# Two eighths of a V unit are kept across the layers, and parts of w_down lie elsewhere

## Chip, core and metric

The kernel runs on one core of one Trainium2 chip. The metric is the device time of one execution in microseconds, as the median of several runs. The profile is of one execution; its times are microseconds from the start of the span.

## What is computed

Two blocks are applied in turn, twice: x grows by grouped-query attention over a cached K and V, then by a SwiGLU feed-forward block (FFN). Both layers use the same weights and the same caches. There is one query token in each of 4 batches.

```python
B, Sq, D = 4, 1, 512
Hq, Hkv, Sk, Dh = 32, 8, 8192, 128        # A: attention, all bfloat16
F = 1792                                  # B: FFN

def _A_ref(x, k_cache, v_cache, wq, wo):
    q = (x @ wq).reshape(B, Sq, Hq, Dh).transpose(0, 2, 1, 3)
    k = jnp.repeat(k_cache, rep, axis=1)
    v = jnp.repeat(v_cache, rep, axis=1)
    scores = jnp.einsum("bhqd,bhkd->bhqk", q, k) * (Dh ** -0.5)
    p = _softmax(scores, axis=-1)
    o = jnp.einsum("bhqk,bhkd->bhqd", p, v)
    return o.transpose(0, 2, 1, 3).reshape(B, Sq, Hq * Dh) @ wo

def _B_ref(x, w_gate, w_up, w_down):
    return (_silu(x @ w_gate) * (x @ w_up)) @ w_down

x = A_x
x = x + _A_ref(_layernorm(x), ...)
x = x + _B_ref(_layernorm(x), ...)
x = x + _A_ref(_layernorm(x), ...)
x = x + _B_ref(_layernorm(x), ...)
```

## The kernel before

**Units and slots.** K and V are cut into 16 units (NP), each a pair of KV heads of one batch. K(L, u) and V(L, u) are the 4 MB of unit u that layer L reads. A unit fills one slot of SBUF, 32 KB in each of 128 partitions. There are four slots (0 to 3), and a fifth, QS, which holds wq until layer 1's projection is done and K or V after that. A slot has eight parts of 512 KB (NB = 8, `BW` elements wide; the code's index q), named `s<slot>.<q>`. They are called eighths here, and pairs where two are meant. All lie in the one tensor `kvf`, so the profile's DMA rows show `kvf` for K, V and the FFN's weights alike.

**Order of units.** Layer 0 takes units 0 to 15. Layer 1 takes 15, 14, 13, 12 and then 0 to 11, because some of the last units of layer 0 are still there: K(15), V(15) and V(14) whole (`keep`), and the last two eighths of K(13), which stand in PSUM during the FFN (`hold`).

**Loads.** All loads are issued by the sync engine (SP) from one list, `cmds`, strictly in order; `pump` issues the next one as soon as the parts of the slot that it fills are in `free`. `freed` adds parts and calls `pump`; it is called where the code emits the last reader of these parts, and SP itself then waits on semaphores for that reader. Every load and every recorded operation goes through `_Sync`, so the trace shows SP's loads on one line, L93.

**A unit's work.** DVE turns K with 32-bit transposes in its place (`turn`, L488; two eighths at a time except for the first and last unit of a layer). PE makes scores (`scores`, L512: four matmuls for an eighth), which ends with `finished`, and so frees the eighth. When the eighth eighth is scored, DVE takes the maximum (`max_p`, L518), PE transposes it (`max_t`, L523), and DVE, PE and ACT go on to the exponentials (`exps`). DVE turns the probabilities into the tile `pT` (`turn_p`, L576), and PE multiplies them with V (`values`, L644; half of the unit's V at a time is freed). Each engine runs its instructions in the order in which they are emitted. PE's work stands in the list `blocks`, and `drain(lag)` emits from its front while more than `lag` us (by the code's own estimates, 0.9 for a block) stand in it; the lag is `LAG` (2.0), and `AHEAD` for the second unit of layer 1. DVE's turns are emitted at once, and so ahead of the PE blocks in the list, and of the DVE work that those blocks call for.

**The change of layers.** The weights of layer 0's FFN are loaded into slot 1 (`W_SLOT[0]`) when V(0,13) has been used there. In elements of a partition: w_gate at 0 to 7168, the rest of w_up to 9216 (the larger part of w_up has a place of its own, `wres`), w_down's 14 blocks of 512 up to 16384, the slot's end. The last two of these (12 and 13) come late, by the command `W+`: their place holds the turned probabilities of the layer's last unit (`late_pT`), which POOL sets to zero first. Then `ffn` frees slot 1 piece by piece, and K(1,14) is loaded into these pieces: eighths 0 to 2 after the gate's matmuls (L882), 3 after w_up's, 4 and 5 after w_down's first eight blocks (L913), 6 and 7 after the rest. K(1,13) goes to QS, in two commands, after the projection (L841) and after what was held in PSUM is turned back (L453). K(1,12) goes to slot 0 in pairs as K(1,15) is scored there, and V(1,13) to slot 1 in two halves as K(1,14) is scored.

```python
cmds += [(("W", 0), W_SLOT[0], 0, NB), (("W+", 0), W_SLOT[0], NB, NB + 1)]
cmds += [(K(1, us[1]), s, a, b) for a, b in ((0, 3), (3, 4), (4, 6), (6, NB))]
cmds += [(K(1, us[2]), QS, 0, NB // 2), (K(1, us[2]), QS, NB // 2, NB - 2)]
cmds += placed(seq, ring, {0: twos, 1: half, len(seq) - 1: ends})
```

Of the kernel before, what the change touches and what calls it, by code (L numbers as in the profile page):

```python
# [9 lines left out]
FP32 = mybir.dt.float32  # L10
# [93 lines left out]
def bass_interleave_layers__gqa_block_cached__swiglu_ffn__decode_kernel(  # L104
# [40 lines left out]
    with ExitStack() as es:  # L145
# [13 lines left out]
        wo_sb = sb("wo_sb", [P, Hq, D], BF16)  # L159
        WDS = (((0, 8, 4), (8, 12, 4), (12, 14, 2)), ((0, 8, 2), (8, 12, 2), (12, 14, 2)))  # L160
        NW = len(WDS[0])

        W_SLOT = (1, 3)
        O_WU = KT * F
        O_WD = O_WU + KT * F - RES
        assert O_WD + FO * D <= SL
        wres = kvf[:, (NSLOT + 1) * SL:]

# [18 lines left out]
        def wd_at(s, fo, k):  # L187
            return columns(s * SL + O_WD + fo * D + pick2(k).start)

        pT_w = TB * NH * QB  # L190
        assert all((w[-1][1] - w[-1][0]) * D >= pT_w for w in WDS)

        def late_pT(s):
            return kvf[:, (s + 1) * SL - pT_w:(s + 1) * SL]

# [18 lines left out]

        pT = sb("pT", [P, TB, NH, QB], BF16)

        pb = sb("pb", [P, SW], BF16)
# [135 lines left out]
        for n, i in ((4, 0), (7, 1), (10, 2), (13, 3)):  # L353
            cmds.insert(n, (("wo", i), None, 0, 0))
        cmds += [(("W", 0), W_SLOT[0], 0, NB), (("W+", 0), W_SLOT[0], NB, NB + 1)]

        us = order[1]
        s = W_SLOT[0]
        cmds += [(K(1, us[1]), s, a, b) for a, b in ((0, 3), (3, 4), (4, 6), (6, NB))]
        cmds += [(K(1, us[2]), QS, 0, NB // 2), (K(1, us[2]), QS, NB // 2, NB - 2)]  # L360
        seq = loads(1, 3)
        ring = (0, 1, 3, QS, 2)
        cmds += placed(seq, ring, {0: twos, 1: half, len(seq) - 1: ends})
        assert W_SLOT[1] == ring[len(seq) % len(ring)]
        cmds += [(("W", 1), W_SLOT[1], 0, NB), (("W+", 1), W_SLOT[1], NB, NB + 1)]

        free = {(s, q) for s in range(NSLOT) for q in range(NB)}
# [3 lines left out]
        def load_weight(name, i=0, s=0):  # L371
# [5 lines left out]
            elif name == "wo":  # L377
                src = A_wo[i * H2 * Dh:(i + 1) * H2 * Dh, :]
                T.dma("sp", wo_sb[:, i * H2:(i + 1) * H2, :].rearrange("p (c j) n -> p c (j n)", j=NA),
                      src.rearrange("(c p j) n -> p c (j n)", p=P, j=NA), sem_w["wo"][i], writes=[f"wo{i}"])  # L380
            else:
                w0 = kvf[:, s * SL:(s + 1) * SL]
                if name == "W+":
                    load_wd(w0, i, NW - 1, ["late"])
                    return
                T._wait("pool", T._need((), [f"s{s}.{NB - 1}"]))
                T.op("pool", lambda e: e.memset(late_pT(s).bitcast(FP32), 0.0), writes=["late"])
                T.dma("sp", w0[:, 0:KT * F].rearrange("p (c x) -> p c x", c=2),
                      B_w_gate.rearrange("(c p e) f -> p c (e f)", c=2, e=2), sem_w["wg"][0],
                      writes=[f"s{s}.{q}" for q in range(NB)] + ["wg"])  # L390
                up = B_w_up.rearrange("(c p e) f -> c p (e f)", c=2, e=2)
                if i == 0:
                    T.dma("sp", wres[:, 0:2 * F], up[0], sem_w["wu"][0], writes=["wu0"])
                    T.dma("sp", wres[:, 2 * F:], up[1, :, 0:FY], sem_w["wu"][1], writes=["wu1"])
                T.dma("sp", w0[:, O_WU:O_WD], up[1, :, FY:], sem_w["wu"][2], writes=["wu2"])

                for j in range(NW - 1):
                    load_wd(w0, i, j)

        def load_wd(w0, L, j, also=()):  # L400
            a, b, e_ = WDS[L][j]
            T.dma("sp", w0[:, O_WD + a * D:O_WD + b * D].rearrange("p (m x) -> p m x", x=e_ * D),
                  B_w_down[a * P:b * P, :].rearrange("(m p e) n -> p m (e n)", p=P, e=e_), sem_w["wd"][j],
                  writes=[f"wd{j}"] + list(also))

        def pump(most=len(cmds)):
            while issued[0] < most:
                it, s, a, b = cmds[issued[0]]
                if it[0] == "wo":
                    load_weight(*it)  # L410
                else:
                    need = {(s, q) for q in range(a, b)}
                    if not need <= free:
                        return
                    free.difference_update(need)
                    if it[0] in ("W", "W+"):
                        load_weight(it[0], it[1], s)
                    else:
                        slot_of[it] = s
                        load(it, a, b, sem_s[s] if b - a == NB else part_sem())  # L420
# [4 lines left out]
        def load(it, a, b, sm):  # L425
            kind, L, u = it
            s = slot_of[it]
            gp, bt = pair_gb(u)
            src = (A_k_cache if kind == "K" else A_v_cache)[bt, 2 * gp:2 * gp + 2, :, :].rearrange(
                "h (p t) d -> (h p) (t d)", t=TT)  # L430
            over = [w for i, w in enumerate(WQ) if s == QS and a // (NB // 2) == i and w not in q_gone]
            q_gone.update(over)
            T.dma("sp", kv[:, s, a * BW:b * BW], src[:, a * BW:b * BW], sm,
                  writes=[f"s{s}.{q}" for q in range(a, b)] + over)

# [23 lines left out]
        def finished(it, a, b):  # L459
# [3 lines left out]
            if it in keep:  # L463
                slot_of[keep[it]] = slot_of[it]
                if it[0] == "K":
                    turned.update((1, it[2], q) for q in range(a, b))
            else:
                freed(slot_of[it], a, b)

# [14 lines left out]
        def turn(L, u, q, n):  # L484
            s = slot_of[K(L, u)]
            w = kv[:, s, q * BW:(q + n) * BW].bitcast(FP32)
            names = [f"s{s}.{i}" for i in range(q, q + n)]
            T.op("dve", lambda e: e.transpose(w, w), reads=names, writes=names)  # L488
# [16 lines left out]
        def scores(L, u, q):  # L505

            s = slot_of[K(L, u)]
            bk = SBK[turn_of[u]]
            w = kv[:, s, q * BW:(q + 1) * BW].rearrange("p (t c i e) -> p t c i e", t=TB, c=2, e=2)
            for c in range(4):  # L510
                z0 = ZP + c * P - REP * q
                T.op("pe", lambda e: e.matmul(bank(bk)[:, 0:SW], lhsT=zq[:, z0:z0 + P], rhs=w[:, :, c // 2, :, c % 2],  # L512
                                              start=(q == 0 and c == 0), stop=(q == NB - 1 and c == 3)),
                     reads=[f"s{s}.{q}", "zq"], writes=[f"pb{bk}"], sig=(c == 3))

# [50 lines left out]
        def pT_of(L, u):  # L566
            if u == order[L][-1]:
                return late_pT(W_SLOT[L]).rearrange("p (t n x) -> p t n x", n=NH, x=QB), "late"
            return pT[:], "pT"
# [17 lines left out]
        LAG = 2.0  # L587
        AHEAD = 15.0

# [37 lines left out]
        def values(L, u):  # L627
# [22 lines left out]
            def part(i):  # L650
# [18 lines left out]
                if i == 3:  # L669
                    more = later.pop(0)() if later else []  # L670
                    if p_name == "late":
                        freed(W_SLOT[L], NB, NB + 1)
                    done.add((L, u))
                    if last:
# [190 lines left out]
        def ffn(L):  # L865
# [5 lines left out]
            rb = rstd[:].unsqueeze(1).to_broadcast([P, FO, B])  # L871
            rooms = {"wg": room(s, 0, O_WU), "wu": room(s, O_WU, O_WD)}
            for j, (a, b, _) in enumerate(WDS[L]):
                rooms[f"wd{j}"] = room(s, O_WD + a * D, O_WD + b * D)
            names = {"wg": ["wg"], "wu": ["wu0", "wu1", "wu2"]}
            for at, wname, bk in ((wg_at, "wg", gb), (wu_at, "wu", ub)):
                for fo in range(FO):
                    if bk == gb and fo == FO // 2:
                        deviation(zero_sb, "zero")
                    f = base(L, fo)  # L880
                    for kt in range(KT):
                        T.op("pe", lambda e: e.matmul(bank(bk)[:, fo * B:(fo + 1) * B],  # L882
                                                      lhsT=at(s, kt, *f),
                                                      rhs=xn[:, kt * B:(kt + 1) * B],
                                                      start=(kt == 0), stop=(kt == KT - 1)),
                             reads=rooms[wname] + names[wname] + ["xn"], writes=[f"pb{bk}"],
                             sig=(fo == FO - 1 and kt == KT - 1))
                freed(s, *((0, 3) if wname == "wg" else (3, 4)))
            T.op("dve", lambda e: e.tensor_tensor(fb(gr), fb(gT), rb, ALU.mult),
# [19 lines left out]
            for j, (a, b, _) in enumerate(WDS[0]):  # L909
                k = OBK[0] if j else SBK[1]  # L910
                for nt in range(KT):
                    for fo in range(a, b):
                        T.op("pe", lambda e: e.matmul(bank(k)[:, nt * B:(nt + 1) * B],  # L913
                                                      lhsT=wd_at(s, fo, nt),
                                                      rhs=hT[:, fo * B:(fo + 1) * B],
                                                      start=(j < 2 and nt == 0 and fo == a),
                                                      stop=(j in (0, NW - 1) and nt == KT - 1 and fo == b - 1)),
                             reads=["hT", f"wd{j}"] + rooms[f"wd{j}"], writes=[f"pb{k}"], sig=(fo == b - 1))
                if not j:
                    freed(s, 4, 6)  # L920
                    add_to_x(bank(k)[:, 0:XB], f"pb{k}")
            freed(s, 6, NB)
            add_to_x(bank(k)[:, 0:XB], f"pb{k}")
# [80 lines left out]
```

## Time and profile before

| | us |
|---|---|
| median of 3 runs | 646.91 |
| fastest, slowest | 646.84, 648.01 |
| the profiled execution | 647.03 |
| its span | 645.1 |
| busy in it: DVE, PE, ACT, POOL | 422.0, 419.5, 41.2, 11.1 |
| last load (w_down of layer 1) landed | 642.4 |

Read the table with the span: an engine that is busy 65% of it need not set its length. A DMA row of the profile gives the issue's start on SP; a landing is the time at which the transfer's semaphore has its last of sixteen steps, one for each DMA engine. The issues around the change of layers, with their landings from the trace:

| issued | landed | KB | what |
|---|---|---|---|
| 323.96 to 325.37 | 341.77 to 346.19 | 3584 | w_gate, w_up |
| 326.78, 327.64 | 348.76, 350.02 | 1024, 512 | w_down 0 to 7, 8 to 11 |
| 338.15 | 350.66 | 256 | w_down 12, 13 (`W+`) |
| 345.22 | 354.34 | 1536 | K(1,14) 0 to 2 |
| 348.30 | 355.61 | 512 | K(1,14) 3 |
| 349.88 | 358.10 | 1024 | K(1,14) 4, 5 |
| 351.11 | 360.56 | 1024 | K(1,14) 6, 7 |
| 354.51, 356.64 | 365.47, 367.95 | 2048, 1024 | K(1,13) 0 to 3, 4 and 5 |
| 361.31, 363.05, 364.80, 366.54 | 370.45, 372.91, 375.40, 377.86 | 1024 each | K(1,12) in pairs |
| 372.18, 375.66 | 382.76, 387.65 | 2048 each | V(1,13) in halves |
| 377.84 | 397.37 | 4096 | K(1,0) |
| 389.02 | 407.09 | 4096 | V(1,12) |

### The profile page before, as it was taken

The numbers are of one execution on the slowest core, as the hardware profiler recorded it, in microseconds if no ns is written. First come the engines' busy times: TensorE is split into PE (matmuls) and PEld (weight loads), VectorE is DVE, ScalarE is ACT, GpSimd is POOL, SyncE is SP. The second block draws the span as 40 slices with busy tenths as digits, with TensorE's granted clock in tenths as the row PEclk, the third lists the DMA queues.
The fourth block names the chain that finished last, engine by engine and source line by source line (L and its number), as shares of the span: only waits on it lengthen the run. The fifth ranks groups of instructions, "written<-read, shape, count | busy, mean of one in ns | idle before, by whom it ended". The sixth has DMA issues, their size and how long they took to land.

```text
span 645.1 us, 7412 instructions
## 1 busy us (share of the span) xinstructions
PE 419.5 (65%) x3126; PEld 182.6 (28%) x3128; DVE 422.0 (65%) x591; ACT 41.2 (6%) x117; POOL 11.1 (2%) x43
## 2 busy tenths in 40 slices
PE   0683475456765746767867877777555676557877
PEld 0431122122222312222226433233122222222325
DVE  5275467456776656776962778878655677665964
ACT  0000000000000000000010010000000000000110
POOL 0000000000000000000000000000000000000000
PEclk9995887688876889767975899997778887679787
DMA  9999999999999999999999999999999999999997
GB/s 368 442 425 418 440 434 425 426 433 438 425 425 440 433 424 432 435 431 424 433 412 404 424 446 424 425 438 432 425 428 443 424 427 439 432 427 426 441 410 276
DMA packets 14704, 273.36 MB, mean 424 GB/s; under 512 B 1480, under 2 KB 1488, under 8 KB 5328
## 3 DMA queue, kind: packets, MB, share of 16 engines
q1 hardware_dynamic: 14672, 272.91, 99.1%
q8 instruction: 24, 0.39, 0.2%
q14 instruction: 8, 0.07, 0.0%
HBM read 272.90 MB, written 0.00 MB: 423 GB/s over the span
## 4 chain that ended last, share of the span: by engine, by line
DMA 62%; DVE 20%; PE 12%; issue 3%; another core or an unknown queue 1%; SPq 0%; ACTq 0%; ACT 0%; DVEq 0%
DMA kvf<-in_A_k_cache_dram 50%; DVE kvf L488 16%; DMA kvf<-in_A_v_cache_dram 11%; PE ps L512 7%; PE ps L644 2%; DMA kvf<-in_B_w_down_dram 2%; DVE pb L694 2%; PE ps L841 1%; PE ps L882 0%; DVE pb L690 0%; DVE kvf L453 0%; DVE scr L704 0%; SPq L93 0%; PE ps L523 0%
## 5 line engine op out<-in xcount | busy, mean ns | idle before, releaser
L512 PE MATMUL ps<-kvf,zq 128*128 128x512 bf16 x1024 | 297.0, 437 | 182.0 <-DVE kvf L488 178.2
L488 DVE STREAM_TRANSPOSE kvf<-kvf 128x2048 f32<-128x2048 f32 (+1 forms) x131 | 280.0, 2162 | 127.8 <-DMA kvf<-in_A_k_cache_dram 127.6
L512 PEld LDWEIGHTS ps<-kvf,zq 128*128 128x128 bf16 x1024 | 100.7, 109 | 339.7 <-DVE kvf L488 218.7
L644 PE MATMUL ps<-kvf,pT 128*32 128x512 bf16 x960 | 65.8, 396 | 1.3 <-DVE pT L576 1.3
L559 ACT ACTIVATE pb<-ps,tiny 128x512 bf16<-128x512 f32 x32 | 22.0, 688 | 529.7 <-DVE tiny L557 510.0
L576 DVE STREAM_TRANSPOSE pT<-pb 64x512 bf16<-64x512 bf16 x60 | 41.2, 687 | 3.6 <-ACT pb L559 2.6
L694 DVE SCALAR_TENSOR_TENSOR pb<-ps,tiny,pb 128x128 f32<-128x128 f32 x104 | 36.5, 351 | 4.5 <-PE ps L644 0.8
L518 DVE TENSOR_REDUCE tiny<-ps 128x1 f32<-128x512 f32 x32 | 22.0, 687 | 21.3 <-PE ps L512 21.3
L644 PEld LDWEIGHTS ps<-kvf,pT 128*32 128x32 bf16 x960 | 20.8, 98 | 31.0 <-issue 15.3
L699 PEld LDWEIGHTS ps<-sel,pb 128*128 128x128 f32 x64 | 17.3, 278 | 16.6 <-DVE pb L694 8.0
L502 POOL TENSOR_TENSOR zq<-scr,tiny 128x64 bf16<-128x64 bf16 x30 | 9.0, 299 | 563.3 <-PE ps L512 563.3
L526 DVE TENSOR_REDUCE mrm<-ps 1x8 f32<-1x128 f32 x32 | 8.8, 275 | 13.8 <-PE ps L523 13.8
L549 PEld LDWEIGHTS ps<-mrm,tiny 128*128 128x128 f32 x60 | 13.7, 234 | 9.6 <-issue 3.3
L699 PE MATMUL ps<-sel,pb 128*128 128x8 f32 x64 | 12.5, 269 | 5.5 <-DVE pb L694 5.5
L841 PE MATMUL ps<-xn,kvf 128*128 128x4 bf16 x256 | 7.4, 166 | 11.3 <-DMA kvf<-in_A_wq_dram 11.0
L549 PE MATMUL ps<-mrm,tiny 128*128 128x16 f32 x60 | 10.4, 251 | 3.1 <-ACT mrm L561 3.1
L690 DVE TENSOR_SCALAR pb<-ps,tiny 128x128 f32<-128x128 f32 x32 | 10.1, 316 | 2.6 <-PE ps L644 2.6
L760 PE MATMUL ps<-wo_sb,scr 128*4 128x512 bf16 x48 | 11.0, 379 | 0.4 <-DVE scr L729 0.4
L841 PEld LDWEIGHTS ps<-xn,kvf 128*128 128x128 bf16 x256 | 7.3, 105 | 11.6 <-DMA kvf<-in_A_wq_dram 11.2
L523 PE MATMUL ps<-identf,tiny 128*1 128x128 f32 x32 | 8.6, 270 | 1.9 <-DVE tiny L518 1.9
L561 ACT ACTIVATE mrm<-head,tiny 128x8 f32<-128x8 f32 x32 | 9.6, 300 | 1.0
L882 PE MATMUL ps<-xn,kvf 128*128 128x4 bf16 x224 | 7.3, 169 | 1.6 <-DMA kvf<-in_B_w_up_dram 1.2
(83 smaller groups left out, 113.1 us busy)
## 6 DMA issues: line engine op xcount, KB each, us to landing
kvf<-in_A_k_cache_dram SPq DMA_DIRECT2D x27, 4096.0 KB, 31.0
kvf<-in_A_v_cache_dram SPq DMA_DIRECT2D x27, 4096.0 KB, 35.3
kvf<-in_A_v_cache_dram SPq DMA_DIRECT2D x4, 2048.0 KB, 18.4
kvf<-in_A_k_cache_dram SPq DMA_DIRECT2D x7, 1024.0 KB, 9.9
kvf<-in_A_k_cache_dram SPq DMA_DIRECT2D x3, 2048.0 KB, 11.0
kvf<-in_A_wq_dram SPq DMA_DIRECT2D x2, 2048.0 KB, 18.1
wo_sb<-in_A_wo_dram SPq DMA_DIRECT2D x4, 1024.0 KB, 41.3
kvf<-in_B_w_gate_dram SPq DMA_DIRECT2D x2, 1792.0 KB, 23.7
```

The costliest lines, as they stand in the source:

```text
L488: T.op("dve", lambda e: e.transpose(w, w), reads=names, writes=names)
L512: T.op("pe", lambda e: e.matmul(bank(bk)[:, 0:SW], lhsT=zq[:, z0:z0 + P], rhs=w[:, :, c // 2, :, c % 2], start=(q == 0 and c == 0), stop=( ...
L518: T.op("dve", lambda e: e.tensor_reduce(mx[:], bank(bk)[:, 0:SW], AX.X, ALU.max), reads=[f"pb{bk}"], writes=["mx"])
L549: T.op("pe", lambda e: e.matmul(at, lhsT=ones, rhs=mrm[:, i * H2:(i + 2) * H2], start=True, stop=True), reads=[f"m8{i}", "rsm", "onesf"], ...
L559: T.op("act", lambda e: e.activation(pb[:], bank(bk)[:, 0:SW], ACTF.Exp, bias=nm, accum_out=rs), reads=[f"pb{bk}", "nm"], writes=PB + ["rs"])
L576: T.op("dve", lambda e: e.transpose(dst, pb[hp]), reads=["pb", "row"], writes=[name])
L644: T.op("pe", lambda e: e.matmul(bank(k)[j * QB:(j + 1) * QB, q0 * Dh:q1 * Dh], lhsT=p_t[:, t, h, :], rhs=v[:, q0:q1, t, :], start=((last o ...
L690: T.op("dve", lambda e: e.tensor_scalar(into, o, own[:, q:q + 1], None, op0=ALU.mult), reads=[f"pb{k}", "own"], writes=["row"] if last els ...
L694: T.op("dve", lambda e: e.scalar_tensor_tensor(into, o, own[:, q:q + 1], into, op0=ALU.mult, op1=ALU.add), reads=[f"pb{k}", "own", iname], ...
L699: T.op("pe", lambda e: e.matmul(at, lhsT=into, rhs=sel[:], start=True, stop=True), reads=[iname, "sel"], writes=[name])
L760: T.op("pe", lambda e: e.matmul(bank(OUTB)[0:B, 0:D], lhsT=oT[:, h, :], rhs=wo_sb[:, h, :], start=(gp == groups[L][0] and r == 0), stop=(g ...
L841: T.op("pe", lambda e: e.matmul(at[:, h * B:(h + 1) * B], lhsT=wq_sb[:, kt, h * Dh:(h + 1) * Dh], rhs=xn[:, kt * B:(kt + 1) * B], start=(k ...
```

## The change

Eighths 6 and 7 of V(0,13) stay in slot 1 and are read by layer 1's V(1,13) (`parked`, `PARK` = 6). Of V(1,13) only eighths 0 to 5 are loaded. The FFN's weights of layer 0 then have six eighths of slot 1 in place of eight. w_down's blocks 8 to 13 stand at 9216 to 12288; blocks 6 and 7 go to the tile `pT` (command `Wp`, after V(0,14)'s last products); blocks 0 to 5 go over the first half of w_gate (command `W2`, two transfers, after the gate's matmuls have used that half). For this the gate's matmuls run in two passes, over kt 0 and 1 for all columns and then over kt 2 and 3, and w_down is added up in the order 8 to 11, 12 and 13, 6 and 7, 0 to 3, 4 and 5. POOL sets `pT` to zero again after blocks 6 and 7 are used. K(1,14) is loaded in the order 2; 3; 4 and 5; 0 and 1; its eighths 6 and 7 go to the first two eighths of slot 0 (`aside`, `home`), after K(1,13), when K(1,15) has been scored there. K(1,12)'s first pair, which shares that place, is loaded after V(1,13). `AHEAD` is 10.9 in place of 15.0.

```diff
-        WDS = (((0, 8, 4), (8, 12, 4), (12, 14, 2)), ((0, 8, 2), (8, 12, 2), (12, 14, 2)))
+        WDS = (((8, 12, 4), (12, 14, 2), (6, 8, 2), (0, 4, 4), (4, 6, 2)), ((0, 8, 2), (8, 12, 2), (12, 14, 2)))
+        PARK = NB - 2
+        ENDS = (PARK * BW, SL)
+        LATE = (1, 2)
+        FO_P, FO_S = WDS[0][2][:2]
...
         def wd_at(s, fo, k):
-            return columns(s * SL + O_WD + fo * D + pick2(k).start)
+            o = pick2(k).start
+            if FO_P <= fo < FO_S:
+                o += (fo - FO_P) * D
+                return pTf[:, o:o + 2 * (P - 1) + 1:2]
+            return columns(s * SL + wd_from(0, fo) + o)
+
+        def wd_from(L, fo):
+            return O_WD + fo * D if L else fo * D if fo < FO_P else O_WD + (fo - FO_S) * D
...
-        cmds += [(("W", 0), W_SLOT[0], 0, NB), (("W+", 0), W_SLOT[0], NB, NB + 1)]
+        parked = {V(0, NP - 3): V(1, NP - 3)}
+        cmds += [(("W", 0), W_SLOT[0], 0, PARK), (("Wp", 0), W_SLOT[0], NB + 1, NB + 2),
+                 (("W+", 0), W_SLOT[0], NB, NB + 1)]
...
-        cmds += [(K(1, us[1]), s, a, b) for a, b in ((0, 3), (3, 4), (4, 6), (6, NB))]
+        cmds += [(("W2", 0), s, NB + 2, NB + 3)]
+        cmds += [(K(1, us[1]), s, a, b) for a, b in ((2, 3), (3, 4), (4, PARK), (0, 2))]
         cmds += [(K(1, us[2]), QS, 0, NB // 2), (K(1, us[2]), QS, NB // 2, NB - 2)]
+        cmds += [(K(1, us[1]), 0, PARK, NB)]
         seq = loads(1, 3)
         ring = (0, 1, 3, QS, 2)
-        cmds += placed(seq, ring, {0: twos, 1: half, len(seq) - 1: ends})
+        rest = placed(seq, ring, {0: twos, 1: lambda it, s: [(it, s, 0, QH), (it, s, QH, PARK)],
+                                  len(seq) - 1: ends})
+        cmds += rest[1:6] + rest[:1] + rest[6:]
...
+        aside = K(1, us[1])
+
+        def home(it, a, b):
+            if it == aside and a >= PARK:
+                return 0, a - PARK, b - PARK
+            return slot_of[it], a, b
...
+                if name == "Wp":
+                    load_wd(pTf, i, 2, ["pT"])
+                    return
+                if name == "W2":
+                    load_wd(w0, i, 3, ["wg0"])
+                    load_wd(w0, i, 4)
+                    return
...
+            elif it in parked and b > PARK:
+                slot_of[parked[it]] = slot_of[it]
+                freed(slot_of[it], a, PARK)
             else:
-                freed(slot_of[it], a, b)
+                freed(*home(it, a, b))
...
-        AHEAD = 15.0
+        AHEAD = 10.9
...
+                    if (L, u) == (0, NP - 2):
+                        freed(W_SLOT[L], NB + 1, NB + 2)
...
-            for at, wname, bk in ((wg_at, "wg", gb), (wu_at, "wu", ub)):
+            for at, wname, bk, ks in ((wg_at, "wg0", gb, (0, KT // 2)), (wg_at, "wg1", gb, (KT // 2, KT)),
+                                      (wu_at, "wu", ub, (0, KT))):
                 for fo in range(FO):
-                    if bk == gb and fo == FO // 2:
-                        deviation(zero_sb, "zero")
                     f = base(L, fo)
-                    for kt in range(KT):
+                    for kt in range(*ks):
...
-                freed(s, *((0, 3) if wname == "wg" else (3, 4)))
+                if wname == "wg0":
+                    deviation(zero_sb, "zero")
+                    if not L:
+                        freed(s, NB + 2, NB + 3)
+                else:
+                    freed(s, *((0 if L else 2, 3) if wname == "wg1" else (3, 4)))
...
-                k = OBK[0] if j else SBK[1]
+                k = OBK[0] if j > 2 else SBK[1]
...
-                if not j:
-                    freed(s, 4, 6)
+                if j == 1:
+                    freed(s, 4, PARK)
+                if j == 2:
                     add_to_x(bank(k)[:, 0:XB], f"pb{k}")
-            freed(s, 6, NB)
+                    T.op("pool", lambda e: e.memset(pTf.bitcast(FP32), 0.0), writes=["pT"])
+            freed(s, 0, 2)
             add_to_x(bank(k)[:, 0:XB], f"pb{k}")
```

## Prediction

> **What bounds the kernel now.** I read the page's slices first, then the busy times by stretch around the change of layers, then single DMA issues with their landings, then the timeline behind them.
>
> ```profile
> span 645.1 us, 7412 instructions
> DMA  9999999999999999999999999999999999999997
> GB/s 368 442 425 418 440 434 425 426 433 438 425 425 440 433 424 432 435 431 424 433 412 404 424 446 424 425 438 432 425 428 443 424 427 439 432 427 426 441 410 276
> HBM read 272.90 MB, written 0.00 MB: 423 GB/s over the span
> ```
>
> The DMA engines are busy in every slice up to the tail, at 404 to 446 GB/s, while PE and DVE each stand idle a third of the span. So the transfers set the end, and a byte not read is time, as long as no DMA engine runs out of work. Whether one does is decided in the change of layers:
>
> ```profile
> core 0: us, PE busy (x) PEld busy (x) DVE busy (x) ACT busy (x) POOL busy (x), PEclk, DMA share, GB/s
> 340.00:350.00 10.00, 6.88 (x180) 6.57 (x180) 2.83 (x14) 0.81 (x3) 0.00 (x0) 0.50 1.03 413
> 350.00:360.00 10.00, 8.26 (x178) 6.33 (x179) 3.88 (x12) 0.56 (x2) 0.00 (x0) 0.50 1.02 411
> 360.00:370.00 10.00, 8.73 (x39) 3.40 (x36) 9.64 (x7) 0.00 (x0) 0.30 (x1) 0.94 0.99 416
> 370.00:380.00 10.00, 8.26 (x62) 3.35 (x61) 5.67 (x10) 1.08 (x3) 0.30 (x1) 1.00 1.02 428
> ```
>
> The share is still 1.0 in all four, but here the queue is shortest. Two single issues show how short (start of the issue, and time from it to the landing):
>
> ```profile
> L93 SPq DMA_DIRECT2D kvf<-in_A_k_cache_dram x1: 328/328/328, 348.3 to 348.3; - x1
> ...
> DMA to landing us min/median/max: 7.3/7.3/7.3
> L93 SPq DMA_DIRECT2D kvf<-in_A_v_cache_dram x1: 328/328/328, 372.2 to 372.2; - x1
> ...
> DMA to landing us min/median/max: 10.6/10.6/10.6
> ```
>
> Over the kernel a 4 MB issue lands 31.0 us (K) or 35.3 us (V) later, by the page's medians; here it is 7 to 11 us. The last view is the work that decides when those issues can be made:
>
> ```profile
> 360.19 8.85 DVE L488 STREAM_TRANSPOSE kvf<-kvf 128x2048 f32<-128x2048 f32 x4
> 368.96 0.65 DVE L518 TENSOR_REDUCE tiny<-ps 128x1 f32<-128x512 f32 x1
> 369.67 0.27 PE L523 MATMUL ps<-identf,tiny 128*1 128x128 f32 x1 [0.72 <-DVE tiny L518]
> 372.18 3.81 SPq L93 DMA_DIRECT2D kvf<-in_A_v_cache_dram  x2
> ```
>
> DVE turns the four pairs of eighths of K(1,14), then takes the maximum of K(1,15)'s scores; PE, in order, waits for that, and K(1,14)'s scores behind it free the room for V(1,13).
>
> **Part 1, bytes.** V(1,13) is read as 3 MB instead of 4. Its two halves of 2 MB landed at 382.76 and 387.65, so 2 MB take 4.89 us and 1 MB **2.45 us**. All of it lies on the path.
>
> **Part 2, more and smaller transfers.** K(1,14) goes from 1536 + 512 + 1024 + 1024 KB (landed 3.68, 1.27, 2.49 and 2.46 us after the one before: 9.90) to two of 512 and three of 1024 KB: 2 x 1.27 + 3 x 2.47 = 9.95. w_down goes from 1024 + 512 + 256 KB (2.57 + 1.26 + 0.64 = 4.47) to two of 512 and three of 256: 2 x 1.26 + 3 x 0.64 = 4.44. V keeps two transfers. Together +0.02, I take +0.05 us. On SP it is three more issues of 0.33 to 0.46 us, and SP waits for buffers most of the time. A rule of the Trainium skill speaks against it: DMA: Bandwidth & Descriptors (Bandwidth; Anatomy of one DMA) asks for at least 1 MiB a transfer and fits 2.0 us fixed to each on the GpSimd path; by that, three more cost 6 us. The 256 KB transfer landing 0.64 us after its forerunner disagrees, as that cost is hidden while others are queued.
>
> **Part 3, the FFN's order.** The gate's 56 matmuls stay 56, in two runs of 28 (1.07 and 1.01 us now). The first run ends at 343.85; w_down's blocks 0 to 5, now over the first half of w_gate, are issued then (two issues, to 344.8). The weights before them landed until 350.66 less their own 1.26 + 0.64, so 348.75: the queue is full, and they land at 350.65, where the last weight landed before. Behind them wait the down matmuls, then x, the projection and all of layer 1. Now those end at 351.07, after landings at 350.02 and 350.66; afterwards also near 351.1: **0**, covered by 3.5 us of queue. Blocks 6 and 7 go to pT after V(0,14)'s last products (about 332.5), 16 us before use: 0. POOL's new memset of pT (0.53 us for such a one) is off the path: its next work starts at 366.65, and pT's next writer at 372.23. AHEAD's new value changes nothing: at most ten blocks of 0.9 (9.0) stand in that list there, under 10.9 as under 15.0.
>
> **Part 4, a new wait.** K(1,14)'s last pair now goes to slot 0 behind K(1,13), after K(1,15)'s first two eighths are scored: issued at 361.31, where K(1,12)'s first pair is now, which landed at 370.45. With 1 MB less ahead it lands at 370.45 - 2.45 = 368.0. DVE wants it at 366.8 (360.19 + 3 x 2.2): it waits 1.2 to 1.3 us. Behind it on DVE stand the maximum, on PE the scores from K(1,14)'s third eighth on, and V(1,13)'s first half is issued not at 372.18 but at **373.45**.
>
> **Part 5, does the queue run dry?** From 348.3 on, every issue finds 1 MB (2.45 us) less ahead of it. An engine with nothing queued starts 1.0 us after an issue (first issue 0.74, first packet 1.75). The sixteen engines are not level: of the sixteen completions of the transfer before V(1,13) the first came at 375.02, the last at 377.86; nine lie within 1.2 us of the first, seven at 2.4 to 2.85. A completion trails the packets by 0.35 us (8.17 against 7.83).
> For the slowest engine, spare time = landing before it - 2.45 - 0.35 - (issue + 1.0): at 348.30 it is 354.34 - 3.80 - 348.30 = 2.2; at 354.51 it is 360.56 - 3.80 - 354.51 = 2.2; at V(1,13), 377.86 - 3.80 - 373.45 = **0.6**. It never stops. The nine fast engines do, up to 2 us, and come out of it within 0.6 us of the slowest, at 2.25 on the scale where the slowest has 2.85. What they lose counts only if one later becomes the slowest. Until 632 the slow ones gain about 1.55 (to 4.4 at the last weight), and one of the nine gains two delays, 1.2 to 2.4 (by 397) and on to 3.9 (by 554), 2.7 in all: 2.25 + 2.7 = 4.95 against 4.4, so **+0.5 us**. If delays fall on other engines it is between 0 and, for two on the slowest (2.85 + 2.7 - 4.4), 1.1.
>
> Later slots: K(1,12)'s first pair lands at 387.65 - 2.45 = 385.2 and is turned at 390.46 now; 5 us spare. V(1,12)'s issue at 389.02 + 1.3 has 397.37 - 3.80 - 390.3 = 3.3 us. After that the queue only grows.
>
> **Sum.** -2.45 + 0.05 + 0 + 0.5 = -1.9. The profiled execution had a span of 645.1 and 647.03 us in all, 0.12 over the median 646.91 of the runs (646.84 to 648.01). So 645.1 - 1.9 = 643.2 span, and **645.0 us** on the median's scale. 1.3 us (0.2%) is what a measurement here tells from nothing.
>
> **Rivals.**
> 1. The queue does run dry on all engines. V(1,13)'s first half has 0.6 us; each 1 us later costs 1 us. For: a chain of DVE, PE and SP stands before it. Against: each link is a row. One to two us more: 646.0 to 647; middle **646.4**. Chance 0.13.
> 2. PE runs at half clock behind Part 4's wait. PE would stand 2.0 us (368.95 to 370.95) instead of 0.72. L512 matmuls took 0.43 us behind a gap of 1.91 at 300.8, but 0.22 behind gaps of 1.74 at 379.5 and 3.18 at 438.6: open. Eight such before the issue: +1.7, of which 1.1 is beyond the spare, and the engines then level, with the 2.7 on top: 1.55 - 2.7 eats 1.15 more. -2.4 + 1.1 + 1.15: **646.7**. Chance 0.08. (The Trainium skill, TensorE: Matmul & The Clock Gate, What's actually happening, wants an idle window of about 3.4 us for half clock; by it, no loss here. The 1.91 row is against it.)
> 3. Slower: DVE's wait for K(1,14)'s last pair. Break-even is an issue of V(1,13) at 376.5 (377.86 - 0.35 - 1.0), so a landing of the pair 3.05 us after 368.0, at 371.05. If slot 0 came free so late that the pair took the place of the transfer after (372.91 now), 1.85 us are lost: **648.8**. For: DVE is 9.64 of 10 us busy there and cannot catch up. Against: K(1,15)'s scores need none of this. Chance 0.09.
> 4. The bytes don't fall, because the parked eighths are read again: **646.9**, chance 0.02; 272.90 MB read would show it.
> 5. The three more transfers cost what an unqueued one does: 1.0 us before its first packet and 0.35 us behind its last (Part 5), 4.0 us for three: **649.0**, chance 0.02. The 0.64 us row is against it. (By the Trainium skill's 2.0 us each, the page of Part 2, it would be 651; that row is against it too.)
>
> **Numbers.** Forecast 0.66, own range 644.1 (nothing lost to uneven engines, 0.4 for a luckier spread of delays) to 645.7 (all 1.1 lost, rounded). The rest as above. Faster: 0.66. Within 0.2%: rivals 1, 2 and 4, 0.23. Slower: rivals 3 and 5, 0.11. The range for 8 in 10 goes from 0.1 under the own range's end over rivals 1, 2 and 4, with 0.3 for the spread of the runs above them: 644.0 to 647.2; rivals 3 and 5 and a little at both ends are left out.
>
> **What would show it.** HBM read 271.85 MB. The last FFN weight of layer 0 landing at 350.6, the down matmuls ending near 351.1. A gap of DVE before the fourth L488 of K(1,14), 1.2 us, ended by a K landing at 368. V(1,13)'s first issue near 373.4. DMA share under 1.0 between 345 and 375, back to 1.0 from 380. The last landing near 640.5 instead of 642.44. Wrong is the forecast if V(1,13)'s issue comes after 374, if w_down's blocks land after 351, or if the last landing moves by less than 1.3 us.

## The result, and the profile after

| | before | changed |
|---|---|---|
| median, us | 646.91 (9 runs) | 648.99 (9 runs) |
| fastest, slowest | 646.73, 648.01 | 647.44, 649.68 |
| span of the profiled execution | 645.1 | 647.3 |
| HBM read, MB | 272.90 | 271.85 |
| last load landed | 642.44 | 644.59 |

The changed kernel takes 1.0029 of the time before, with a 95% interval of 1.0018 to 1.0039: 2.1 us more, where 1.9 us less were forecast. The bytes fell as said. First the page of the changed kernel: span, DMA share and rate in 40 slices, and what was read.

```profile
span 647.3 us, 7423 instructions
DMA  9999999999999999999999989999999999999997
GB/s 373 436 421 423 449 421 421 442 429 422 435 435 424 431 437 426 429 439 425 426 414 362 424 363 420 437 434 421 435 431 429 430 435 429 428 436 430 427 417 277
HBM read 271.85 MB, written 0.00 MB: 420 GB/s over the span
```

Two slices that ran at 404 and 446 GB/s before are at 362 and 363 now: the 22nd (340 to 356 us) and the 24th (372 to 388). They are the two places where time is lost. The busy times by stretch show them closer (busy us of PE, PEld, DVE, ACT, POOL, granted clock, DMA share, GB/s), the changed kernel first, then the one before:

```profile
346.00:350.00 4.00, 2.94 (x91) 2.81 (x91) 0.83 (x4) 0.00 (x0) 0.49 (x1) 0.50 0.99 348
350.00:354.00 4.00, 3.05 (x85) 2.80 (x86) 0.96 (x6) 0.00 (x0) 0.04 (x1) 0.50 0.95 328
...
370.00:374.00 4.00, 1.97 (x5) 0.54 (x5) 2.26 (x3) 0.00 (x0) 0.00 (x0) 0.65 1.01 418
374.00:378.00 4.00, 4.00 (x12) 1.68 (x12) 1.58 (x4) 1.08 (x3) 0.00 (x0) 0.50 0.51 160
```

```profile
346.00:350.00 4.00, 2.94 (x88) 2.82 (x88) 0.99 (x4) 0.00 (x0) 0.00 (x0) 0.50 1.06 422
350.00:354.00 4.00, 2.99 (x80) 2.74 (x80) 1.01 (x7) 0.00 (x0) 0.00 (x0) 0.50 0.98 371
...
370.00:374.00 4.00, 4.00 (x20) 1.84 (x19) 1.84 (x5) 1.08 (x3) 0.00 (x0) 1.00 1.02 420
374.00:378.00 4.00, 3.74 (x41) 1.23 (x38) 1.86 (x3) 0.00 (x0) 0.30 (x1) 1.00 1.05 440
```

At 374 to 378 the engines stand half the time. At 346 to 354 the share barely falls, yet the rate drops by 74 and 43 GB/s. The trace's packet records show two reasons. From 344 to 358 an engine is without any packet for 0.60 us in the mean of the sixteen (0.02 before). And a packet that begins on an engine with nothing queued is counted as busy for longer than it needs in a full queue: thirteen packets of 16 KB that began between 377.4 and 378.0 took 1.08 to 1.41 us, where their median over the kernel before is 0.61. PE's clock in the second place is the other thing to see: 0.50, where it was 1.00. The timeline of the changed kernel shows what stood before the second place:

```profile
360.05 6.66 DVE L536 STREAM_TRANSPOSE kvf<-kvf 128x2048 f32<-128x2048 f32 x3
366.89 1.90 PE L560 MATMUL ps<-kvf,zq 128*128 128x512 bf16 x8 [0.55 <-DVE kvf L536]
369.09 2.31 DVE L536 STREAM_TRANSPOSE kvf<-kvf 128x2048 f32<-128x2048 f32 x1 [2.38 <-DMA kvf<-in_A_k_cache_dram]
371.32 0.65 DVE L566 TENSOR_REDUCE tiny<-ps 128x1 f32<-128x512 f32 x1
372.03 0.37 PE L571 MATMUL ps<-identf,tiny 128*1 128x128 f32 x1 [3.24 <-DVE tiny L566]
372.20 1.91 PE L560 MATMUL ps<-kvf,zq 128*128 128x512 bf16 x4
374.56 6.19 PE L560 MATMUL ps<-kvf,zq 128*128 128x512 bf16 x20
376.52 2.89 SPq L93 DMA_DIRECT2D kvf<-in_A_v_cache_dram  x2
```

(L536 is L488 of the kernel before, L560 its L512, L566 its L518, L571 its L523.) DVE waits 2.38 us for K(1,14)'s last pair, PE then 3.24 us for DVE's maximum, and works at half clock afterwards: four matmuls in 1.91 us instead of 1.03, twenty in 6.19 instead of 4.53. V(1,13)'s first half is issued at 376.52 instead of 372.18, to an empty queue.

Where the loss accrues can be followed on the landings, those of the same work side by side. From the second row on, the changed kernel has 1 MB less to load by then, which should have brought 2.45 us:

| | before | changed | difference |
|---|---|---|---|
| last FFN weight of layer 0 | 350.66 | 350.52 | -0.14 |
| K(1,14)'s eighths 4 and 5 | 358.10 | 356.77 | -1.33 |
| K(1,12)'s last pair | 377.86 | 376.61 | -1.25 |
| all that stands before K(1,0) | 387.65 | 388.66 | +1.01 |
| V(1,12) | 407.09 | 409.32 | +2.23 |
| last load | 642.44 | 644.59 | +2.15 |

### The profile page after: what moved, and what is told of

Read it like the earlier page. It is cut to its first block, busy times and chain, and to the rows that moved or that the text cites. A ratio compares the mean times of both kernels' runs of the same rounds, so it can differ in the third digit from the quotient of the medians.

```text
span 647.3 us, 7423 instructions
## 1 busy us (share of the span) xinstructions
PE 420.3 (65%) x3128; PEld 181.6 (28%) x3128; DVE 421.9 (65%) x591; ACT 41.2 (6%) x117; POOL 11.6 (2%) x44
## 3 DMA queue, kind: packets, MB, share of 16 engines
HBM read 271.85 MB, written 0.00 MB: 420 GB/s over the span
## 4 chain that ended last, share of the span: by engine, by line
DMA 61%; DVE 20%; PE 13%; issue 3%; another core or an unknown queue 1%; SPq 1%; ACT 0%; ACTq 0%; DVEq 0%
DMA kvf<-in_A_k_cache_dram 51%; DVE kvf L536 16%; PE ps L560 8%; DMA kvf<-in_B_w_down_dram 6%; DMA kvf<-in_A_v_cache_dram 4%; PE ps L692 2%; DVE pb L744 2%; SPq L93 1%; PE ps L891 1%; DVE pb L740 0%; DVE scr L754 0%; DVE pT L624 0%; PE ps L571 0%; DVE rl L587 0%
## 5 line engine op out<-in xcount | busy, mean ns | idle before, releaser
L560 PE MATMUL ps<-kvf,zq 128*128 128x512 bf16 x1024 | 295.5, 435 | 181.4 <-DVE kvf L536 177.2
L536 DVE STREAM_TRANSPOSE kvf<-kvf 128x2048 f32<-128x2048 f32 (+1 forms) x131 | 280.2, 2162 | 126.8 <-DMA kvf<-in_A_k_cache_dram 126.6
L560 PEld LDWEIGHTS ps<-kvf,zq 128*128 128x128 bf16 x1024 | 100.2, 109 | 339.5 <-DVE kvf L536 220.1
L566 DVE TENSOR_REDUCE tiny<-ps 128x1 f32<-128x512 f32 x32 | 22.0, 687 | 22.3 <-PE ps L560 22.3
L571 PE MATMUL ps<-identf,tiny 128*1 128x128 f32 x32 | 8.7, 273 | 4.4 <-DVE tiny L566 4.4
```

The lines of the kernel that those rows point to most:

```text
L566: T.op("dve", lambda e: e.tensor_reduce(mx[:], bank(bk)[:, 0:SW], AX.X, ALU.max), reads=[f"pb{bk}"], writes=["mx"])
```

## Experiments

The theories: **A**, DVE's wait for K(1,14)'s last pair makes V(1,13)'s issue late and the queue empty at 374. **B**, the loss is made earlier, at 346 to 355, where K(1,14)'s pieces meet a short queue. **C**, more transfers, and engines that have become level, cost it. After the first four runs, three were added. **L**: 1 MB less queue at 345 to 360 lets engines run empty, which takes away what absorbs later delays. **F**: the FFN's new order and the smaller transfers eat the gain. **P**: the slowest engine's delays hide part of 1 MB anywhere.

| run | median, us | ratio to before, 95% interval |
|---|---|---|
| changed, 12 filling matmuls | 648.02 | 1.0020, 1.0011 to 1.0028 |
| changed, 16 filling matmuls | 648.41 | 1.0023, 1.0014 to 1.0032 |
| changed, maximum early | 646.54 | 0.9987, 0.9979 to 0.9996 |
| changed, last pair one transfer later | 652.32 | 1.0092, 1.0075 to 1.0109 |
| before, maximum early | 646.98 | 0.9999, 0.9990 to 1.0008 |
| before, 1 MB less of V(1,5) | 644.71 | 0.9964, 0.9951 to 0.9976 |
| before, 1 MB less of K(1,14) | 646.34 | 0.9989, 0.9981 to 0.9998 |
| before, 1 MB less of V(1,13) | 644.68 | 0.9966, 0.9954 to 0.9979 |
| changed, maximum early, V(1,13) read whole | 648.90 | 1.0028, 1.0017 to 1.0039 |
| before, V(1,5) in eight transfers | 647.58 | 1.0010, 1.0001 to 1.0019 |

### The maximum ahead of the last pair

```diff
-        AHEAD = 10.9
+        AHEAD = 4.0
```

> AHEAD 4.0 puts DVE's maximum of K(1,15) ahead of the turn of K(1,14)'s last pair; loads and PE's order stay. Theory A: V(1,13)'s first half issued near 371.2, DMA share 1.0 from 372 on, 645.7 us (645.2 to 646.5). Theories B and C: 649, since nothing of the loads changes.

DVE's order is the only thing that changes; PE's and SP's instructions and all loads stay. From its timeline and its stretches:

```profile
367.10 0.69 DVE L566 TENSOR_REDUCE tiny<-ps 128x1 f32<-128x512 f32 x1 [2.73 <-PE ps L560]
370.10 2.29 DVE L536 STREAM_TRANSPOSE kvf<-kvf 128x2048 f32<-128x2048 f32 x1
370.74 4.53 PE L560 MATMUL ps<-kvf,zq 128*128 128x512 bf16 x20
371.86 2.07 SPq L93 DMA_DIRECT2D kvf<-in_A_v_cache_dram  x2
```

```profile
350.00:354.00 4.00, 3.04 (x88) 2.79 (x86) 0.96 (x6) 0.00 (x0) 0.00 (x0) 0.50 1.02 385
...
374.00:378.00 4.00, 3.43 (x39) 1.14 (x37) 2.94 (x5) 0.00 (x0) 0.30 (x1) 1.00 1.01 428
```

The issue comes at 371.86, PE keeps its clock, the hole at 374 is gone, and the kernel takes 646.54 us, 2.45 less than the changed one. So A is right for what the change loses against the kernel before. Of the versions here that load all they need, it is the only one whose interval lies below the kernel before, though by 0.4 us only. But A said 645.7 (645.2 to 646.5): 1 MB should bring 2.3 us, and 1.9 us are still missing.

The eleven executions of this run lie between 645.21 and 647.11; the profiled one took 647.11, and its landings show two losses. K(1,14)'s eighths 4 and 5 landed 3.61 us after the transfer before them, where 2.49 is usual. Later, in the transfer that landed at 375.33, fifteen of the sixteen completions were there by 373.59, and the last came 1.74 us behind them, so 1.5 us were lost to one engine. The trace has a packet of 16 KB of the instruction queue (q8 on the page) that began at 371.18 and took 1.09 us; which engine it ran on is not recorded. Before, such a packet began at 370.34, and the last completions there stayed 2.5 us apart.

> The kernel before with AHEAD 4.0. Theory A: its queue has over 4 us to spare at V(1,13)'s first half, so the order on DVE gains nothing: 646.9 (646.6 to 647.2). If the order alone is worth something apart from the queue, it shows here as less than 646.6.

646.98: in the kernel before, the order alone is worth nothing; it is worth 2.45 us only where the queue is short.

### The last pair later still

```diff
-        cmds += [(K(1, us[1]), 0, PARK, NB)]
...
-        cmds += rest[1:6] + rest[:1] + rest[6:]
+        cmds += rest[1:2] + [(K(1, us[1]), 0, PARK, NB)] + rest[2:6] + rest[:1] + rest[6:]
```

> K(1,14)'s last pair is loaded one 1 MB transfer later, after K(1,12)'s second pair. Theory A: it lands 2.5 us later, V(1,13) is issued near 379, and the time grows by the same: 651.5 (650.5 to 652.5). Theories B and C: 649, as bytes, pieces and the FFN's order are the same.

The pair lands at 371.94 instead of 369.07, V(1,13)'s issue comes at 379.09, and the time is 3.3 us over the changed kernel's. B and C, for which it had to stay at 649, are out as the cause of this part. Stretches of this run:

```profile
370.00:374.00 4.00, 0.00 (x0) 0.00 (x0) 2.04 (x1) 0.00 (x0) 0.00 (x0) 0.72 1.01 420
374.00:378.00 4.00, 3.09 (x9) 1.33 (x10) 1.31 (x5) 0.20 (x1) 0.00 (x0) 0.50 0.24 98
378.00:382.00 4.00, 4.00 (x19) 1.67 (x17) 1.41 (x2) 0.88 (x3) 0.00 (x0) 0.93 0.49 152
```

PE has nothing at all to do for 4 us, and the hole in the DMA is twice as long: from 374 on, an engine is without a packet for 5.2 us in the mean, against 2.6 in the changed kernel.

### PE kept busy over its wait

The changed kernel, with matmuls whose results nobody reads put in front of `max_t` of layer 1's first unit (12; in a second run 16):

```diff
+                    warm = 12 if L and u == order[L][0] else 0
-                    line.extend([step(0.0, max_p), step(1.2, max_t)])
+                    line.extend([step(0.0, max_p), step(1.2, lambda u: (stream(warm), max_t(u)))])
```

> Theory A: DVE's wait for K(1,14)'s last pair leaves PE idle 3.2 us, PE then runs at half clock, and V(1,13)'s first half is issued at 376.5 to an empty queue. Twelve matmuls of 0.22 us put into that gap keep the clock up: issue near 374.6, no stretch in which all DMA engines are idle, 646.5 us (645.8 to 647.2). Theory B: the loss is made earlier, at 346 to 355, where K(1,14)'s pieces meet a short queue: 649, as the changed kernel. Theory C: more transfers and levelled engines cost it: 649.

A's 646.5 was missed by 1.5 us. In the profiled execution (649.17, where the median is 648.02) the pair landed later still (369.86) and twelve were too few: the next four scores ran at full clock (1.04 us), the twenty after them at half (6.20), and the issue came at 375.99. So this run does not tell the clock's share.

> As the run with twelve filling matmuls, but sixteen, so that PE is busy until the wait ends and the clock's window from 371.2 to 374.6 is full. If the half clock is a part of the loss: L560 at 0.22 us each from 372 to 378, V(1,13) issued near 374.7, 647.3 us (646.8 to 647.8). If the late landing of K(1,14)'s last pair alone decides: issue after 376, 649.

With sixteen the clock holds, and the issue is where it was expected:

```profile
368.27 3.61 PE L673 MATMUL ps<-wo_sb 128*128 128x512 bf16 x16
371.23 0.65 DVE L566 TENSOR_REDUCE tiny<-ps 128x1 f32<-128x512 f32 x1
373.32 4.53 PE L560 MATMUL ps<-kvf,zq 128*128 128x512 bf16 x20
374.44 2.07 SPq L93 DMA_DIRECT2D kvf<-in_A_v_cache_dram  x2
```

```profile
374.00:378.00 4.00, 4.00 (x22) 1.63 (x24) 1.53 (x3) 0.76 (x3) 0.01 (x1) 1.00 0.81 281
```

The time is not: 648.41, with single runs from 647.22 to 649.46 (the profiled one took 647.67). The issue still comes too late to keep all engines busy, as the second line shows (0.81, 281 GB/s). The half clock is shown to make the issue 2.1 us later. What it costs in time is not shown: the two medians are 0.6 and 1.0 us under the changed kernel's, of the 2.45 that the early maximum brings, but their intervals overlap the changed kernel's.

### One megabyte less, at three places

Three times the kernel before, with 1 MB less to load and nothing else altered; what is not loaded is told in the expectations. These kernels leave out bytes that the computation needs.

```diff
-        cmds += placed(seq, ring, {0: twos, 1: half, len(seq) - 1: ends})
+        cmds += placed(seq, ring, {0: twos, 1: half, len(seq) - 1: ends,
+                                   seq.index(V(1, 5)): lambda it, s: [(it, s, 0, NB - 2)]})
```

> The kernel before, but the last two eighths of V(1,5) are not loaded (its products take what stands there): 1 MB less in the middle of layer 1, where the queue is 14 to 17 MB deep. All theories that call 1 MB worth 2.45 us: 644.5 (644.1 to 644.9). Theory P, that the slowest engine's delays hide part of it anywhere: 645.5 or more.

```diff
-                            load(it, a, b, sem_s[s] if b - a == NB else part_sem())
+                        if (it, a) != (K(1, NP - 2), NB - 2):
+                            load(it, a, b, sem_s[s] if b - a == NB else part_sem())
```

> The kernel before, but the last two eighths of K(1,14) are not loaded (its scores take what stands there): 1 MB less at the change of layers, with the FFN, the transfers and DVE's order as before. Theory L, that 1 MB less queue at 345 to 360 lets the fast engines run empty and so takes away what absorbs later delays: 646.2 (645.7 to 646.6). Theory F, that the new FFN order and smaller transfers ate the gain, and the bytes are worth their time here too: 644.5 (644.1 to 644.9).

```diff
-                        load(it, a, b, sem_s[s] if b - a == NB else part_sem())
+                        if (it, a) == (V(1, NP - 3), NB // 2):
+                            load(it, a, NB - 2, part_sem())
+                        else:
+                            load(it, a, b, sem_s[s] if b - a == NB else part_sem())
```

> The kernel before, but the last two eighths of V(1,13) are not loaded (its products take what stands there): the same 1 MB as the change saves, without its new places. Theory L: 1 MB less at 382 comes after the short stretch of the queue, no engine runs empty for it (the fastest has 4.2 us before V(1,12)'s packets are due, less 2.45), so the full price: 644.6 (644.2 to 645.0). If bytes at the change of layers are worth less in any place: 646.0 or more.

V(1,5): 2.26 us less, so P is out. V(1,13), the very bytes that the change saves: 2.29 us less. K(1,14)'s last pair, which leaves the queue at 351: 0.63 us less. The same megabyte is worth about a quarter there, with the FFN, the number of transfers and DVE's order as before. So L stands. It takes 2.29 - 0.63 = 1.66 us, and the new places cost 1.93 (below); the 0.3 us between them, which would be F's, is less than the intervals tell (0.1 to 1.2 us for the 0.63, 1.1 to 2.5 for the 1.93). One stretch of the run without K(1,14)'s pair, then the same of the run without V(1,13)'s:

```profile
354.00:358.00 4.00, 3.27 (x91) 2.74 (x88) 1.13 (x4) 0.56 (x2) 0.00 (x0) 0.50 1.03 393
```

```profile
354.00:358.00 4.00, 3.27 (x92) 2.75 (x89) 1.10 (x4) 0.56 (x2) 0.00 (x0) 0.50 1.05 435
```

The rate is lower in the first. The sixteen completions of a transfer say what follows: with K(1,14)'s pair left out the time between the first and the last shrinks from 2.62 us (at 357.8) to 1.48 (362.7) and 1.29 (370.6), with V(1,13)'s it stays at 2.6 to 2.7. The engines that were ahead have stood still or been slow until the others caught up. That alone costs nothing yet: at 365 the run without the pair is 2.79 us ahead of the kernel before (landings at 365.16 and 367.95). It loses 0.5 us in the transfer that lands at 368.14, 0.9 in the one at 374.00 and 0.5 in the one at 396.51. Ahead of the last two, packets of the instruction queue began at 371.48 and 394.38. In the run without V(1,13)'s bytes the same two began at 370.14 and 393.70, and cost the last completion 0.1 us and nothing.

### The changed order without the bytes

```diff
-        parked = {V(0, NP - 3): V(1, NP - 3)}
+        parked = {}
...
-        rest = placed(seq, ring, {0: twos, 1: lambda it, s: [(it, s, 0, QH), (it, s, QH, PARK)],
+        rest = placed(seq, ring, {0: twos, 1: lambda it, s: [(it, s, 0, QH), (it, s, QH, NB)],
```

(with AHEAD 4.0)

> The changed kernel with the early maximum (AHEAD 4.0), but nothing kept of V(0,13): V(1,13) is read whole, with the bytes of the kernel before. Theories L and F: 649.0 (648.4 to 649.6), 2.45 over the 646.54 of the kernel with the kept eighths, since the order alone costs 2 us. If the kept bytes were worth nothing here: 646.6.

648.90, as expected by L and F: 2.36 us more than with the kept eighths, so these are worth their price in the run with the early maximum too. The new places cost 1.93 us on their own against the kernel before, with the same bytes and the late issue already mended. This run does not part L from F, as it has the short queue and the FFN's new order both.

### More and smaller transfers

```diff
-        cmds += placed(seq, ring, {0: twos, 1: half, len(seq) - 1: ends})
+        cmds += placed(seq, ring, {0: twos, 1: half, len(seq) - 1: ends,
+                                   seq.index(V(1, 5)): lambda it, s: [(it, s, q, q + 1) for q in range(NB)]})
```

> The kernel before with V(1,5) loaded in eight transfers of 512 KB in place of one of 4 MB, in the deep part of the queue. By the landings, 8 x 1.27 - 9.72 = 0.4 us more: 647.3 (646.9 to 647.7). By an unqueued transfer's 1.35 us for each of seven more: 656.

647.58, 0.61 us more for seven more transfers, 0.09 each. So C's more transfers are out where the queue is deep. The change's three stand where it is short, and no run varied their number alone.

## Why the prediction was wrong

**The price of the bytes (Part 1) was right**: 2.45 us forecast, 2.26 and 2.29 measured in two places, 2.36 in the changed order. Rival 4 is out.

**The transfers (Part 2) were about right**, as far as a run shows them: the rule by landings gave 0.4 us for seven, 0.61 us were measured; the 1.35 us each of rival 5 are out behind a deep queue. The Trainium skill (DMA: Bandwidth & Descriptors, Anatomy of one DMA) fits 2.0 us fixed to each transfer on the GpSimd path; an estimate from that is 14 us for seven, and the 0.61 us measured here, for loads that SP issues behind others, disagree.

**The FFN's order (Part 3) was right for the last completion**: the last weight landed at 350.52 (350.65 forecast), the down matmuls ended at 350.94 (near 351.1), and AHEAD 10.9 gives, instruction for instruction, the program that 15.0 gives. Its "the queue is full" was not right for the engines that were ahead: from 344 to 348, while the late loads of w_down come in, an engine is without a packet for 0.12 us in the mean (0.33 in the run with the early maximum, 0.00 before), so the FFN's order has a part in emptying the queue.

**Part 5 failed first: "For the slowest engine, spare time", "It never stops", and the "+0.5 us" for all the others lose.** The slowest engine had its 2.2 us of spare on paper, yet K(1,14)'s eighths 4 and 5 landed 3.74 us after the transfer before them where 1 MB takes 2.49, and the gain was down to 1.33 us by then. Packets of 8 KB that began there, between 352 and 355, took up to 1.94 us, where 0.31 is their median. The step looked at the engine that was last, as if it stayed the same one. "What they lose counts only if one later becomes the slowest" named the right condition; its size, 0.5 with bounds of 0 and 1.1, was too small. Engines without a queue start slowly, the engines become level, and then a delay of any of them can count. The run with K(1,14)'s pair left out measures it alone, 1.66 us; in the changed order, with what the FFN's order adds, it is 1.93 us.

**Part 4 failed next, and by that**: the last pair landed at 369.07 instead of 368.0, 1.07 us late, so DVE waited 2.38 us and not 1.25.

**Rival 2's mechanism came true on top**: "PE runs at half clock behind Part 4's wait", given 0.08. The wait was longer than the 2.0 us it was weighed at (3.24), and PE worked at half clock until 378. Issue of V(1,13): 373.45 forecast + 1.07 for the later pair + about 2 for the clock = 376.5, measured 376.52.

**The break-even of rival 3 was about 1 us too late.** It put the point from which time is lost at an issue at 376.5. At 376.52, nothing should have been lost against the kernel before; 1.01 us were. The 2 MB landed 7.2 us after their issue, where 4.89 + 1.0 + 0.35 = 6.24 were reckoned. All sixteen engines began from nothing, with the slow first packets told above:

```profile
L93 SPq DMA_DIRECT2D kvf<-in_A_v_cache_dram x1: 328/328/328, 376.5 to 376.5; - x1
...
DMA to landing us min/median/max: 7.2/7.2/7.2
```

The other 1.2 us, up to V(1,12), are one delay of 1.2 us on one engine, seen in its completions: 0.36 us between first and last at 398, 1.58 at 409, where fifteen of the sixteen lie within 0.36 us. A packet of the instruction queue began at 398.86, between the two, and took 1.03 us. Before, such a packet began at 393.95; there were 2.8 us between the completions at that point, and the last ones came 9.72 us apart, as in the transfers after.

In short, by medians: -2.3 for the bytes, +1.9 for the new places and the short queue, +2.45 for the late issue, a sum of +2.05 where +2.08 was measured. The sum has to close, as the runs are steps from one kernel to the other; what they show is the size of each step. The chance of slower, 0.11, was far too small: the loss of Part 5 lay beyond its bounds, and the late pair, the half clock and the empty queue were taken as separate cases, where each leads to the next. The range of 644.0 to 647.2 lacked that.

What stays open: which of the sixteen engines is the last one (the trace does not name them), and so how much of the 1.9 us is slow starts and how much is the loss of the uneven lead; how much of it is the FFN's order; and the exact share of the clock. That a packet of the instruction queue is what delays an engine is a reading of when these packets run, and no run varied them.

## What to carry to other kernels

Where transfers set the end, a byte saved is worth its full time only if the queue around it is deep. A saving that pays with room (two eighths held through a change of stages) shortens the queue exactly where it is shortest; measure that first by leaving the bytes out without moving anything, once at that place and once elsewhere, as here (0.63 against 2.3 us). And where one load has to come later, look at what is emitted in front of its consumer in the same engine's order: to put DVE's maximum ahead of the one transpose that waits was worth 2.45 us, and nothing in the kernel with the deeper queue.

## What the hardware showed that I had not expected

**A busy DMA share is not a rate.** In the changed kernel the share at 350 to 354 is 0.95 at 328 GB/s; in the kernel before a share of 0.98 gave 371, and elsewhere 1.0 gives 420 to 440.

**The lead of fast DMA engines is a store.** In the kernel before the sixteen completions of one transfer lie 0.5 us apart at the start, 3.5 us at 350 and 4.4 us at the end. While it is there, a delay on an engine that is ahead need not move the end, as at 393.95. After the queue has run empty it is 0.4 us, and grows again to 3.0 by the end: 2.6 us, where in the kernel before it grows from 2.9 (at 378) to 4.4, by 1.5. The difference of 1.1 us is close to what the changed kernel loses between 388 and the end (+1.01 to +2.15).

**PE's clock drops after a stretch that is only partly idle.** Half clock was granted for 371.17 to 378.0 in the changed kernel; PE had been busy for about 1 us of the 3.4 us before that. With twelve filling matmuls, half clock was granted for 374.44 to 377.86 and followed a stretch of 3.4 us (371.0 to 374.4) in which PE was busy for 1.8 us, and it lasted while PE worked without a pause. By the Trainium skill (TensorE: Matmul & The Clock Gate, What's actually happening), a window of about 3.4 us decides, and an idle one leads to half clock; the length agrees with the trace, whose two stretches at half clock are 6.83 and 3.41 us long, but here a half-busy one was enough.
